# The list of steps of a second feed-forward exchanged for another list of the same steps

## Chip, core and metric

The kernel runs on one core of a Trainium2 chip. The metric is device time in microseconds from the start to the end of the program; less is better.

## What is computed

Windowed attention with a few global tokens, then a gated feed-forward (mish), then a second feed-forward whose gate is a cosine. Inputs and output are float32; x has 2176 rows of 512, the hidden width is 2048. The second feed-forward is the part that the change touches:

```python
    attn_out = _attn_ref(**attn_kwargs)
    x = np.ascontiguousarray(attn_out.transpose(0, 2, 1, 3)).reshape(B * S, H * D)
    x = _moe_ref(x=x, **moe_kwargs)
    return _moe2_ref(x=x, **moe2_kwargs)

def _moe2_ref(x, w_in, w_out):
    h = x @ w_in
    g = h * np.cos(h)
    return (g @ w_out).astype(np.float32)
```

## The kernel before

Every float32 matmul is made of three fp32r matmuls: each operand is split into a high and a low part, and low x high, high x high and high x low are added in PSUM.

The second feed-forward (`second`, L967) works in 24 stages: two halves p of the hidden width, three blocks b of tokens (2 x 384, 2 x 384, 2 x 320) and four groups j of 256 hidden columns, in that order. Stage s = 12p + 4b + j. In steps such as `P3:11` the number behind the colon is the stage. Within a stage the first matmul (x @ w_in) is done as seven products in place of eight, on sums and differences of the operands' quarters. The steps are:

- A, I, L (L925): form operand o of a token block (number behind the colon: block), cast its high part (I, letter a or d), subtract for the low part and store both to DRAM (L). The operands of one block at a time live in SBUF ("homes").
- P0 to P6 (L1021): product o, six matmuls (L1034) into one of two PSUM banks, chosen by (s + o) mod 2. In stage 4b + 3 a product also issues, on SyncE's queue, the reload of its operand for the next block (L957). At stages 8 to 11 some products also refill weights.
- E0 to E7 (L1048, L1051): copy (E0) or add (L1056, VectorE) a product from its bank, until the four quarters of h are made. A bank is free again when the sum that reads it is done.
- f0 to f6 and g0 to g6 (L1018, L841): the gate on the two column halves c = 0, 1: two ScalarE passes (f0), two VectorE passes (f1, f2), sine and square on ScalarE (f3), a VectorE pass (f4), a cast (f5, letter a or d), a subtraction on VectorE (f6). In the last stage they are cut in two once more (a, b for c = 0; d, c for c = 1). The scratch tile `k` is one for all.
- U0 to U5 and V0 to V5 (L1059): the second matmul (g @ w_out) of column half c = 0 (U) and 1 (V) for 128 tokens a: three matmuls (L1065) of 512 columns that add into PSUM sum a over the four groups j.
- Z0 to Z5 (L1071): empty sum a behind the last group: a copy to `part` for p = 0 (L1081, letter a or d), an add and the store of the output for p = 1 (L1083, L1084).
- X, Y (L1068): the weights of U or V of this stage are used up; for p = 0 at the last block the slot is refilled from DRAM (L433).
- R, S: one quarter each of the last two groups of the first feed-forward's second matmul (L1133).

The letter behind a step puts a copy or cast on ScalarE (a) or VectorE (d), in `move` (L346).

`ORDER2` (L71 to L128) is the order of all of these, written out. The program issues the steps exactly in this order (`tc.manual_schedule()`, L1208; the loop at L1095), so each engine and SyncE's queue gets its instructions in the order of the list and works them off in that order; between engines only data and buffers make one wait for another.

PSUM is full: eight banks. Sums a = 0 and 1 have a tile each, a = 2 and 3 are the two halves of one tile, a = 4 and 5 of another, and two tiles serve the products:

```python
    single = [late["ps"].tile([P, 512], F32, tag="acc", name="acc", bufs=4) for _ in range(4)]
    acc.extend(single[2:4] + [t[:, c] for t in (ps2, ps) for c in range(2)] + single[0:2])
```

In the profile the sums in halves are called `h`, the others `acc`; operands are `xo` and `xq` (o = 5, 6), `stage` where they are formed; h is `hs`, with `u` for partial sums; the gate is `w`, `gh`, `gl`; weights are `w`, `wb`, `wt`, in DRAM `scr`.

Of the kernel before, what the change touches and what calls it, by code (L numbers as in the profile page):

```python
# [68 lines left out]
"""  # L69

ORDER2 = """  # L71
    I6:0d L5:0 I0:1a P0:0 P1:0 E0:0d L6:0 P2:0 R:0 E1:0 I4:1a E2:0 L4:1 P3:0 P4:0 A5:1 E3:0 L0:1 E4:0 A3:1 f0:0
# [4 lines left out]
    P0:3 f0:2 P1:3 f1:2 V5:0 g5:1a E0:3a E1:3 U0:1 A6:1 P2:3 U4:1 f2:2 g6:1 f3:2 P3:3 I6:1d g0:2 U1:1 V1:1 E2:3
    f4:2 P4:3 L6:1 E3:3 E4:3 g1:2 U2:1 g2:2 U3:1 L4:2 U5:1 P5:3 P6:3 V3:1 f5:2a E6:3 g3:2 V0:1 f0:3 E7:3 A5:2 E5:3
    V2:1 P0:4 P1:4 g4:2 g5:2a E0:4a f6:2 V5:1 f1:3 A3:2 U2:2 E1:4 f2:3 P2:4 P3:4 E2:4 U5:2 P4:4 V4:1 U4:2 U0:2 f3:3
    g0:3 I0:2a g6:2 g1:3 E3:4 E4:4 g2:3 U1:2 f4:3 f0:4 g3:3 U3:2 f5:3a P6:4 P5:4 E6:4 E5:4 V5:2 L0:2 E7:4 V0:2 P0:5  # L80
    V4:2 E0:5a g4:3 f6:3 P1:5 g5:3a V3:2 f1:4 E1:5 I1:2d P2:5 P3:5 V1:2 U4:3 f2:4 V2:2 E2:5 I3:2a f3:4 E3:5 P5:5
    P4:5 g6:3 L1:2 L3:2 U0:3 V0:3 f4:4 g0:4 I5:2a U2:3 g1:4 U3:3 g2:4 A2:2 V4:3 V2:3 E4:5 P6:5 g3:4 E5:5 E6:5 E7:5
    g4:4 P0:6 P1:6 U1:3 Z4:3d f0:5 E0:6d U5:3 V1:3 f5:4a E1:6 f6:4 f1:5 A6:2 I2:2d Z0:3a f2:5 g5:4a P2:6 P3:6 E2:6
    f3:5 E3:6 V3:3 Z1:3a U0:4 V5:3 U4:4 P5:6 L5:2 g6:4 P4:6 f4:5 g0:5 V0:4 Z3:3d g1:5 U1:4 U3:4 E6:6 Z5:3a E4:6
    V3:4 E5:6 g2:5 f5:5a I6:2a L6:2 Z2:3a U5:4 P6:6 f0:6 f6:5 V1:4 E7:6 P0:7 U2:4 f1:6 P1:7 E0:7d g3:5 g4:5 L2:2
    P2:7 E1:7 V2:4 f2:6 V4:4 g5:5d E2:7 g0:6 U3:5 f3:6 P3:7 g6:5 P4:7 E3:7 E4:7 g1:6 f4:6 V5:4 g2:6 f5:6d f6:6 U1:5
    U4:5 f0:7 P5:7 g3:6 E6:7 P6:7 f1:7 U0:5 U2:5 E5:7 f2:7 V1:5 f3:7 E7:7 g4:6 V2:5 V0:5 P0:8 U5:5 P1:8 g5:6d E0:8a
    P2:8 f4:7 U0:6 V4:5 E1:8 E2:8 g6:6 P4:8 P3:8 g0:7 g1:7 V3:5 U4:6 E3:8 E4:8 P5:8 V5:5 U1:6 U2:6 g2:7 U5:6 E5:8
    E6:8 P6:8 P0:9 f0:8 g3:7 E7:8 f5:7d f6:7 U3:6 V5:6 f1:8 P1:9 E0:9d f2:8 g4:7 V1:6 V4:6 P2:9 g0:8 U1:7 E1:9
    g5:7d V3:6 g6:7 U4:7 g1:8 E2:9 f3:8 P3:9 P4:9 f4:8 U3:7 E3:9 P5:9 g2:8 V0:6 V2:6 U0:7 E5:9 E4:9 P6:9 f5:8d V3:7  # L90
    g3:8 f0:9 E6:9 E7:9 g4:8 U5:7 P0:10 P1:10 U2:7 f6:8 Z3:7a V1:7 E0:10d V2:7 P2:10 g5:8a E1:10 f1:9 f2:9 Z1:7d
# [6 lines left out]
    V2:10 f1:12 f2:12 E0:13a P1:13 g0:12 P2:13 E1:13 g5:11d P3:13 E2:13 g6:11 V1:10 P4:13 g1:12 V3:10 U1:11 X:8
    E3:13 E4:13 f3:12 V0:10 P5:13 P6:13 U2:11 g2:12 f4:12 E5:13 E6:13 g3:12 E7:13 P0:14 E0:14a P1:14 g4:12 E1:14
    f5:12a V2:11 f0:13 f6:12 P2:14 P3:14 U4:11 V4:11 V1:11 Z4:11a f1:13 U3:11 U0:11 E2:14 Z1:11a V3:11 Y:9 P4:14  # L100
    Z2:11a f2:13 U4:12 E3:14 E4:14 U5:12 P5:14 f3:13 g0:13 g5:12d V0:11 U1:12 U2:12 f4:13 g6:12 P6:14 g1:13 g2:13
# [5 lines left out]
    P0:17 V0:13 E7:16 E0:17a U0:14 P2:17 f5:15a U1:14 g4:15 P1:17 f6:15 U2:14 V1:14 f1:16 E1:17 V5:14 E2:17 f2:16
    P4:17 Y:11 P3:17 V4:14 V0:14 V3:14 E3:17 g5:15d g6:15 f3:16 f4:16 E4:17 P5:17 g0:16 V2:14 Y:20 g1:16 P6:17
    E5:17 E6:17 U3:15 V3:15 g2:16 U1:15 E7:17 U4:15 P0:18 E0:18d P1:18 g3:16 g4:16 U0:15 f5:16d E1:18 P2:18 f0:17
    P3:18 f6:16 V1:15 U5:15 V5:15 U2:15 f1:17 E2:18 f2:17 f3:17 Z1:15 V4:15 E3:18 P5:18 f4:17 P4:18 g0:17 Z4:15  # L110
# [1 line left out]
    g2:17 f5:17d f0:18 f6:17 V4:16 P0:19 V5:16 Z0:15 g3:17 E7:18 f1:18 g4:17 U2:16 U0:16 U5:17 g5:17d f2:18 E0:19a
    V3:16 P2:19 P1:19 U3:17 E1:19 f3:18 f4:18 E2:19 V0:16 P3:19 X:20 U4:17 E3:19 g0:18 g6:17 P4:19 V2:16 g1:18
    E4:19 P5:19 U2:17 g2:18 P6:19 E6:19 U1:17 E5:19 V4:17 f5:18a V5:17 E7:19 g3:18 P0:20 g4:18 f6:18 U0:17 E0:20d
    f0:19 g5:18d P1:20 f1:19 P2:20 E1:20 V0:17 f2:19 P3:20 E2:20 V2:17 f3:19 g6:18 U4:18 E3:20 P4:20 f4:19 P5:20
    E5:20 U5:18 E4:20 E6:20 V1:17 V5:18 V3:17 g0:19 P0:21 Y:22 P6:20 U2:18 g1:19 g2:19 U0:18 E7:20 f5:19d U3:18
    X:21 V3:18 U1:18 V1:18 g3:19 V0:18 P1:21 f0:20 f6:19 E0:21a f1:20 f2:20 P2:21 f3:20 g0:20 g4:19 E1:21 f4:20
    X:22 E2:21 g5:19a P3:21 U5:19 g6:19 V2:18 U1:19 V4:18 E3:21 U0:19 P5:21 E6:21 E5:21 g1:20 U2:19 P4:21 V2:19
    E4:21 g2:20 U4:19 P0:22 P6:21 g3:20 V5:19 U3:19 f0:21 f5:20d f6:20 E7:21 g4:20 P1:22 E0:22a f1:21 V3:19 f2:21
    E1:22 g5:20a Z2:19 X:23 g6:20 P2:22 P3:22 E2:22 V4:19 Z3:19 V1:19 g0:21 P4:22 f3:21 Z1:19 E3:22 Z4:19 V0:19  # L120
    P5:22 E4:22 U2:20 P6:22 U1:20 f4:21 Z0:19 g1:21 f5:21d E6:22 g2:21 U4:20 E5:22 V2:20 U0:20 f6:21 V0:20 P0:23
# [1143 lines left out]
```

## Time and profile before

| | us |
|---|---|
| median of 3 runs (873.9 to 876.3) | 875.49 |
| the profiled run | 875.59 |
| its span, first to last instruction | 873.8 |
| TensorE busy | 859.3 |
| VectorE busy | 731.0 |
| ScalarE busy | 485.4 |

The span is what the trace covers; the run's time has 1.8 us around it. Busy times of the engines overlap. A matmul's row begins when the engine takes it and its end is modelled, so rows of TensorE lie over each other: twelve matmuls in a row last less than twelve times one. An idle time stands in brackets behind an instruction, with the one whose end released it.

### The profile page before, as it was taken

Reading aid. Unit: us, or ns where it says so; the run is one execution under the profiler, and the core shown is the slowest. Engines: PE = TensorE matmul, PEld = TensorE weight load, DVE = VectorE, ACT = ScalarE, POOL = GpSimd, SP = SyncE. Lnnn points to the kernel's source line nnn. Section 1 sums busy time; section 2 is a strip of 40 time slices with the busy share of each in tenths; the row PEclk is TensorE's granted clock in tenths of the full one; section 3 lists DMA queues with packets and bytes.
Section 4 is the critical chain, followed back from the end, with each engine's and each line's share of the span. In section 5 each row is a group of like instructions: output and inputs, shape, how many; then the busy total and the mean of one; then the engine's idle time right before and its main releaser. Section 6 shows DMA issues by size and latency. Waiting matters only on the chain.

```text
span 873.8 us, 16116 instructions
## 1 busy us (share of the span) xinstructions
PE 859.3 (98%) x5995; PEld 790.5 (90%) x5995; DVE 731.0 (84%) x1499; ACT 485.4 (56%) x962; POOL 84.3 (10%) x137
## 2 busy tenths in 40 slices
...
GB/s 170 186 211 173 175 88 81 73 158 229 260 277 270 298 375 345 267 283 268 252 226 238 387 407 211 256 91 151 245 134 335 99 29 344 1 88 196 1 61 72
DMA packets 133886, 174.97 MB, mean 200 GB/s; under 512 B 77872, under 2 KB 100400, under 8 KB 133808
## 3 DMA queue, kind: packets, MB, share of 16 engines
...
## 4 chain that ended last, share of the span: by engine, by line
PE 81%; DMA 8%; DVE 8%; issue 1%; ACT 1%; SPq 0%; DVEq 0%; POOL 0%; POOLq 0%; ACTq 0%
PE acc L1034 17%; PE acc L1133 14%; PE h L1065 13%; PE acc L1065 7%; PE h L810 6%; PE h L812 6%; PE h L811 6%; DMA cs<-in_moe_w_out_dram 3%; DMA cs<-in_moe_w_in_dram 3%; PE s L572 3%; PE av L643 2%; PE ta L616 1%; DVE ca L240 1%; DMA op<-stage 1%; PE av L637 1%
## 5 line engine op out<-in xcount | busy, mean ns | idle before, releaser
L1133 PE MATMUL acc<-gh,w 128*128 128x384 f32 (+1 forms) x768 | 187.9, 328 | 0.0
L1133 PEld LDWEIGHTS acc<-gh,w 128*128 128x128 f32 x768 | 136.5, 189 | 0.0
L1133 PE MATMUL acc<-gl,w 128*128 128x384 f32 (+1 forms) x384 | 126.4, 329 | 3.0 <-DVE x L883 1.9
L810 PE MATMUL h<-x,w 128*128 128x384 f32 (+1 forms) x384 | 126.1, 328 | 0.7 <-DVE x L787 0.7
L812 PE MATMUL h<-x,w 128*128 128x384 f32 (+1 forms) x384 | 125.2, 326 | 0.0
L811 PE MATMUL h<-x,w 128*128 128x384 f32 (+1 forms) x384 | 125.2, 326 | 0.0
L1065 PE MATMUL h<-w,gh 128*128 128x512 f32 x352 | 109.7, 393 | 0.0
L1034 PE MATMUL acc<-xo,w 128*128 128x384 f32 (+1 forms) x402 | 76.3, 327 | 1.6 <-DVE hs L1056 1.6
L1065 PEld LDWEIGHTS h<-w,gh 128*128 128x128 f32 x352 | 66.1, 188 | 11.8
L1133 PEld LDWEIGHTS acc<-gl,w 128*128 128x128 f32 x384 | 72.5, 189 | 4.5 <-DVE x L883 2.2
L856 ACT ACTIVATE w<-w 128x768 f32<-128x768 f32 (+2 forms) x50 | 39.0, 781 | 63.2 <-DVE w L853 63.1
L1034 PEld LDWEIGHTS acc<-xo,w 128*128 128x128 f32 x402 | 68.1, 188 | 6.4 <-DVE hs L1056 2.7
L810 PEld LDWEIGHTS h<-x,w 128*128 128x128 f32 x384 | 72.1, 188 | 1.1 <-issue 1.0
L811 PEld LDWEIGHTS h<-x,w 128*128 128x128 f32 x384 | 72.1, 188 | 0.0
L812 PEld LDWEIGHTS h<-x,w 128*128 128x128 f32 x384 | 72.1, 188 | 0.0
L1065 PE MATMUL h<-w,gl 128*128 128x512 f32 x176 | 69.2, 393 | 1.9 <-DVE part L348 1.0
L1056 DVE TENSOR_TENSOR hs<-u,acc 128x384 f32<-128x384 f32 (+1 forms) x91 | 47.4, 526 | 27.9 <-PE acc L1034 26.5
L846 ACT ACTIVATE k<-hs,magic 128x768 f32<-128x768 f32 (+2 forms) x50 | 43.5, 871 | 49.1 <-DVE w L853 43.0
L1065 PE MATMUL acc<-w,gh 128*128 128x512 f32 x192 | 59.9, 393 | 0.0
L592 ACT ACTIVATE pr<-pr,nm 128x160 f32<-128x160 f32 x128 | 53.5, 423 | 8.8 <-DVE nm L589 8.0
L850 DVE SCALAR_TENSOR_TENSOR w<-k,hs 128x768 f32<-128x768 f32 (+2 forms) x50 | 44.1, 881 | 8.5 <-ACT k L847 6.8
L837 DVE TENSOR_TENSOR gl<-w,gh 128x768 fp32r<-128x768 f32 (+1 forms) x48 | 43.9, 916 | 7.1 <-ACT gh L833 7.1
...
## 6 DMA issues: line engine op xcount, KB each, us to landing
w<-scr SPq DMA_DIRECT2D x44, 512.0 KB, 7.1
scr<-co SPq DMA_DIRECT2D x31, 512.0 KB, 3.3
x<-x SPq DMA_DIRECT2D x32, 384.0 KB, 5.8
...
cs<-in_moe_w_in_dram SPq DMA_DIRECT2D x22, 512.0 KB, 4.3
cs<-in_moe_w_out_dram SPq DMA_DIRECT2D x22, 512.0 KB, 4.2
scr<-lab SPq DMA_DIRECT2D x21, 512.0 KB, 3.8
...
```

Source lines behind the costliest of these rows:

```text
L592: nc.scalar.activation(out=pr[:, i], in_=pr[:, i], func=AF.Exp, bias=nm[:, i:i + 1], scale=-1.0, accum_out=l[:, i:i + 1])
L810: nc.tensor.matmul(ps[:, c, 0:n], wh[:, k, :], xl, start=(k == 0), stop=False)
L811: nc.tensor.matmul(ps[:, c, 0:n], wh[:, k, :], xh, start=False, stop=False)
L812: nc.tensor.matmul(ps[:, c, 0:n], wl[:, k, :], xh, start=False, stop=(k == NK - 1))
L837: nc.vector.tensor_tensor(out=gl, in0=v["w"], in1=gh.bitcast(F32), op=ALU.subtract)
L846: nc.scalar.activation(out=k[:, y], in_=of("h")[:, z], func=AF.Identity, scale=INV2PI, bias=magic[:, 0:1])
L850: nc.vector.scalar_tensor_tensor(out=of("t")[:, z], in0=k[:, y], scalar=-C1, in1=of("h")[:, z], op0=ALU.mult, op1=ALU.add)
L856: nc.scalar.activation(out=of("t")[:, z], in_=of("t")[:, z], func=AF.Sin, scale=0.5)
L1034: nc.tensor.matmul(to, l[:, i + c], r, start=c == 0 and m == 0, stop=c == 1 and m == 2)
L1056: nc.vector.tensor_tensor(out=of[out](), in0=of[x](), in1=bank(s, o), op=ALU.add)
L1065: nc.tensor.matmul(singles()[a], l[:, a * P:(a + 1) * P], r, start=(j, c) == (0, 0) and m == 0, stop=(j, c) == (3, 1) and m == 2)
L1133: nc.tensor.matmul(o[:, 0:n], w[:, a * P:(a + 1) * P], r[:, c, :], start=(not goes_on and g == 0 and m == 0), stop=(not stays and g == G - ...
```

## The change

`ORDER2` is replaced as a whole. Both lists have 1079 steps, and each step of one is in the other; their order differs, and for some the letter a or d. Nothing else in the program changes, the attention's list `ORDER` included. Of the lists those lines that hold the steps spoken of below:

```diff
-    I6:0d L5:0 I0:1a P0:0 P1:0 E0:0d L6:0 P2:0 R:0 E1:0 I4:1a E2:0 L4:1 P3:0 P4:0 A5:1 E3:0 L0:1 E4:0 A3:1 f0:0
-    A2:1 R:1 f1:0 P5:0 R:2 S:0 E6:0 E5:0 f2:0 f3:0 S:1 S:2 P6:0 f4:0 E7:0 f5:0d P0:1 E0:1a f6:0 I3:1a R:3 S:3 g0:0
-    P2:1 P1:1 E1:1 P3:1 E2:1 I1:1a E3:1 g1:0 U2:0 P4:1 P5:1 g2:0 E4:1 L1:1 f0:1 U3:0 E5:1 P6:1 E6:1 L3:1 U5:0 g3:0
...
-    E2:10 f3:9 P3:10 E3:10 g0:9 f4:9 P4:10 P5:10 V4:7 E4:10 g6:8 V5:7 V0:7 U3:8 P6:10 g1:9 g2:9 V3:8 Z2:7d E6:10
-    E5:10 E7:10 Z0:7a Z4:7d P0:11 f5:9a P1:11 U1:8 U0:8 g3:9 f0:10 E0:11a g4:9 f6:9 U2:8 E1:11 P3:11 U4:8 g5:9a
...
-    f4:11 g3:11 P6:12 P5:12 U0:10 E6:12 E5:12 f5:11d f0:12 U3:10 f6:11 E7:12 Z5:7d Y:8 P0:13 g4:11 V4:10 U2:10
...
-    V5:12 E5:14 g3:13 E6:14 P0:15 E7:14 Z3:11d Z0:11d V2:12 U3:12 P1:15 E0:15d f5:13a f0:14 U0:12 X:9 g4:13 f6:13
-    V0:12 f1:14 E1:15 P2:15 E2:15 V3:12 V1:12 f2:14 P3:15 g5:13d Y:10 E3:15 U5:13 P4:15 g6:13 g0:14 P5:15 g1:14
...
-    Z3:15 Y:21 V2:15 U3:16 E4:18 Z5:15 g5:16a g6:16 V0:15 E5:18 E6:18 Z2:15 P6:18 U1:16 g1:17 V1:16 U4:16 U5:16
...
-    V4:21 P6:23 a0:23 g4:22 a1:23 b0:23 E6:23 E7:23 U3:22 V1:21 b1:23 a2:23 U2:21 V0:21 b2:23 g5:22d U0:22 a3:23
-    c0:23 g6:22 b3:23 V2:21 U4:22 d0:23 c1:23 b4:23 V0:22 U2:22 a4:23 b5:23d U1:22 a5:23a d1:23 V4:22 V2:22 d2:23
...
-    Z5:19 U3:23 V0:23 Z2:23 Z4:23 U1:23 V1:23 Z0:23 Y:23 V3:23 Z1:23 Z3:23
+    P0:0 I6:0a L6:0 E0:0a P1:0 P2:0 E1:0 I4:1d E2:0 L5:0 P3:0 P4:0 E3:0 R:0 P5:0 L4:1 E4:0 A5:1 P6:0 E5:0 E6:0 f0:0
...
+    P2:1 P3:1 E2:1 P4:1 f6:0 E3:1 g3:0 U1:0 E4:1 g4:0 I3:1a P5:1 E6:1 U5:0 f0:1 E5:1 P6:1 f1:1 E7:1 P0:2 f2:1 P1:2
...
+    Z2:3a f3:5 Z3:3a E2:6 Z4:3a E3:6 P4:6 E4:6 P5:6 P6:6 E6:6 V5:3 f4:5 V0:3 g0:5 g6:4 U4:4 E7:6 I2:2a U3:4 Z5:3a
+    Z0:3a g1:5 L2:2 f5:5d V3:4 U5:4 U0:4 E5:6 P0:7 U2:4 g2:5 V4:4 g3:5 g4:5 P1:7 E0:7a V2:4 f6:5 E1:7 U1:4 f0:6
...
+    f4:6 L6:2 V1:5 P5:7 g4:6 f0:7 E6:7 V0:5 U5:5 P6:7 U4:5 g5:6a E5:7 P0:8 f5:6d V3:5 f6:6 E7:7 f1:7 f2:7 g6:6 g0:7
...
+    P6:9 U4:7 V5:7 U3:7 f0:9 f5:8d P0:10 E7:9 f6:8 f1:9 f2:9 E0:10a g5:8d V2:7 V4:7 f3:9 f4:9 P1:10 P2:10 Z2:7a
+    V3:7 E1:10 g0:9 V1:7 g6:8 Z4:7a E2:10 P3:10 P4:10 V0:7 E3:10 Z1:7d E4:10 U2:8 g1:9 f5:9a P5:10 Z3:7a P6:10 U1:8
...
+    V0:9 f6:10 g2:10 U2:9 P5:11 V2:9 E4:11 g3:10 E5:11 U4:9 g4:10 E6:11 V4:9 P6:11 g5:10d Z5:7d f0:11 P0:12 E7:11
+    f1:11 V1:9 P1:12 E0:12d f2:11 E1:12 P2:12 E2:12 V3:9 P3:12 P4:12 E3:12 P5:12 g0:11 g6:10 U4:10 X:9 U2:10 E4:12
...
+    P3:14 E2:14 E3:14 U3:11 P4:14 E4:14 P5:14 P6:14 g5:12d E5:14 Z1:11a E6:14 V3:11 E7:14 P0:15 g0:13 Z2:11d f5:13a
+    U0:12 g6:12 Z3:11a U3:12 P1:15 U1:12 E0:15a X:11 f6:13 U2:12 g1:13 Y:11 Z4:11a g2:13 g3:13 U4:12 V4:12 g4:13
...
+    g1:17 U5:16 f3:17 P4:18 P5:18 V5:16 Z3:15 g2:17 E4:18 X:21 f4:17 V4:15 Z1:15 g3:17 V2:15 E6:18 P6:18 U0:16
...
+    P5:23 b1:23 V2:21 b2:23 g4:22 U2:22 g5:22a a1:23 E5:23 a2:23 V1:21 E6:23 b3:23 g6:22 V0:21 a3:23 c0:23 U0:22
+    E7:23 b4:23 Z5:19 U1:22 d0:23 V3:21 d1:23 c1:23 a4:23 V4:21 V0:22 b5:23d U4:22 c2:23 U3:22 V3:22 d2:23 c3:23
...
+    U1:23 Z2:23 Z3:23 U0:23 V0:23 V1:23 V4:23 Z0:23 Z1:23 Z4:23
```

## Rows read from the trace of the kernel before

**Rows 1.** Page: busy us, share of the span, instructions of each engine.
```profile
PE 859.3 (98%) x5995; PEld 790.5 (90%) x5995; DVE 731.0 (84%) x1499; ACT 485.4 (56%) x962; POOL 84.3 (10%) x137
```

**Rows 2.** Busy time by stretch: length, each engine's us, PEclk, DMA share, GB/s.
```profile
530.00:560.00 30.00, 30.00 (x153) 26.95 (x152) 29.19 (x42) 19.95 (x25) 0.00 (x0) 1.00 0.70 265
```

**Rows 3.** Chain that ended last: start, us to the next piece, what.
```profile
538.20 1.39 PE h L1065 x6
539.59 2.10 PE acc L1034 x12
...
808.98 1.75 PE acc L1034 x12
```

**Rows 4.** Waits of TensorE, 495 to 874 us: us in total, times, longest.
```profile
PE acc L1034 <- DVE hs L1056: 2.4, 2, 1.6
PE h L1065 <- DVE part L348: 1.0, 1, 1.0
PE h L1065 <- DMA w<-scr: 0.7, 1, 0.7
PE h L1065 <- DVE part L1083: 0.3, 1, 0.3
```

**Rows 5.** Timeline around U3:0 and P6:1: start, us, engine, line, [idle before <-releaser].
```profile
521.74 0.96 DVE L850 SCALAR_TENSOR_TENSOR w<-k,hs 128x768 f32<-128x768 f32 x1 [1.00 <-ACT k L847]
...
522.51 0.39 PE L1065 MATMUL h<-w,gl 128*128 128x512 f32 x1
...
524.21 1.32 PE L1034 MATMUL acc<-xq,w 128*128 128x384 f32 x6 [0.84 <-DVE hs L1056]
```

**Rows 6.** Waits of ScalarE, 495 to 874 us: us in total, times, longest.
```profile
ACT stage L350 <- DMA op<-stage: 8.4, 6, 3.7
```

**Rows 7.** Timeline: V3:8 begins, finish Z2:7, P0:11 begins.
```profile
654.75 0.39 PE L1065 MATMUL h<-w,gl 128*128 128x512 f32 x1
...
655.64 0.69 DVE L348 COPY part<-h 128x512 f32<-128x512 f32 x1 [1.92 <-PE h L1065]
...
657.18 2.02 PE L1034 MATMUL acc<-xo,w 128*128 128x320 f32 x12 [1.57 <-DVE hs L1056]
```

**Rows 8.** Timeline: P0:13 and V4:10; P4:18 and V2:15.
```profile
685.99 1.23 PE L1034 MATMUL acc<-xo,w 128*128 128x384 f32 x6
...
688.21 0.50 PE L1065 MATMUL h<-w,gl 128*128 128x512 f32 x1 [0.99 <-DVE part L348]
...
773.50 1.21 PE L1034 MATMUL acc<-xo,wt 128*128 128x384 f32 x6
...
774.97 0.50 PE L1065 MATMUL h<-w,gl 128*128 128x512 f32 x1 [0.27 <-DVE part L1083]
```

**Rows 9.** Timeline: P3:15 and U5:13.
```profile
724.12 1.21 PE L1034 MATMUL acc<-xo,w 128*128 128x384 f32 x6
...
725.99 0.50 PE L1065 MATMUL h<-w,gl 128*128 128x512 f32 x1 [0.66 <-DMA w<-scr]
```

**Rows 10.** DMA issues, 495 to 874 us: count, KB each, median us to landing.
```profile
w<-scr SPq DMA_DIRECT2D x24, 512.0 KB, 7.3
...
xq<-op SPq DMA_DIRECT2D x12, 384.0 KB, 6.6
```

**Rows 11.** Groups by line and shape, 495 to 874 us: busy us, mean ns | idle before.
```profile
L348 DVE COPY part<-h 128x512 f32<-128x512 f32 x6 | 4.1, 685 | 1.9 <-PE h L1065 1.9
...
L350 ACT COPY part<-h 128x512 f32<-128x512 f32 x5 | 2.9, 583 | 7.8 <-PE h L1065 7.8
```

**Rows 12.** Timeline at the end: the last gate products (d6, c6), V4:23.
```profile
863.00 1.10 DVE L866 TENSOR_TENSOR gl<-w,gh 128x320 fp32r<-128x320 f32 x2
...
865.20 0.39 PE L1065 MATMUL h<-w,gl 128*128 128x512 f32 x1
```

**Rows 13.** Groups by line and shape: a half-width pass on VectorE.
```profile
L866 DVE TENSOR_TENSOR gl<-w,gh 128x320 fp32r<-128x320 f32 x4 | 1.9, 486 | 0.1
```

**Rows 14.** Waits of SyncE's queue, 495 to 874 us: us in total, times, longest.
```profile
SPq L965 <- DMA op<-stage: 6.7, 1, 6.7
```

More of the change, by code (lines that the diff above doesn't have):

```diff
@@ L77 @@
[L77 to L91, printed above, removed]
@@ L92 @@
-    E2:10 f3:9 P3:10 E3:10 g0:9 f4:9 P4:10 P5:10 V4:7 E4:10 g6:8 V5:7 V0:7 U3:8 P6:10 g1:9 g2:9 V3:8 Z2:7d E6:10
-    E5:10 E7:10 Z0:7a Z4:7d P0:11 f5:9a P1:11 U1:8 U0:8 g3:9 f0:10 E0:11a g4:9 f6:9 U2:8 E1:11 P3:11 U4:8 g5:9a
-    P2:11 f1:10 V1:8 E2:11 f2:10 V4:8 E3:11 g6:9 P4:11 V0:8 g0:10 U3:9 U1:9 P5:11 U0:9 g1:10 E4:11 f3:10 g2:10
-    P6:11 U4:9 g3:10 g4:10 V4:9 f4:10 V2:8 f5:10a V1:9 f0:11 E5:11 E6:11 P0:12 E7:11 V0:9 f6:10 E0:12a P1:12 P2:12
-    f1:11 U4:10 f2:11 U2:9 E1:12 E2:12 P3:12 g5:10a g6:10 P4:12 E3:12 V2:9 g0:11 V3:9 E4:12 g1:11 g2:11 U1:10 f3:11
@@ L97 @@
-    f4:11 g3:11 P6:12 P5:12 U0:10 E6:12 E5:12 f5:11d f0:12 U3:10 f6:11 E7:12 Z5:7d Y:8 P0:13 g4:11 V4:10 U2:10
[L98 to L101, printed above, removed]
@@ L102 @@
-    V5:12 E5:14 g3:13 E6:14 P0:15 E7:14 Z3:11d Z0:11d V2:12 U3:12 P1:15 E0:15d f5:13a f0:14 U0:12 X:9 g4:13 f6:13
-    V0:12 f1:14 E1:15 P2:15 E2:15 V3:12 V1:12 f2:14 P3:15 g5:13d Y:10 E3:15 U5:13 P4:15 g6:13 g0:14 P5:15 g1:14
-    U0:13 U1:13 E4:15 f3:14 f4:14 E6:15 g2:14 E5:15 U3:13 P6:15 E7:15 g3:14 g4:14 P0:16 U2:13 V2:13 V4:12 f5:14a
-    P1:16 E0:16d P2:16 V1:13 U4:13 E1:16 V4:13 f0:15 X:10 g5:14a P3:16 X:11 f6:14 E2:16 f1:15 f2:15 P4:16 g0:15
-    E3:16 f3:15 g6:14 P5:16 U4:14 V5:13 E4:16 V3:13 g1:15 U5:14 U3:14 g2:15 f0:16 P6:16 f4:15 g3:15 E6:16 E5:16
@@ L107 @@
[L107 to L110, printed above, removed]
-    Z3:15 Y:21 V2:15 U3:16 E4:18 Z5:15 g5:16a g6:16 V0:15 E5:18 E6:18 Z2:15 P6:18 U1:16 g1:17 V1:16 U4:16 U5:16
@@ L112 @@
[L112 to L121, printed above, removed]
@@ L127 @@
-    Z5:19 U3:23 V0:23 Z2:23 Z4:23 U1:23 V1:23 Z0:23 Y:23 V3:23 Z1:23 Z3:23
+    P0:0 I6:0a L6:0 E0:0a P1:0 P2:0 E1:0 I4:1d E2:0 L5:0 P3:0 P4:0 E3:0 R:0 P5:0 L4:1 E4:0 A5:1 P6:0 E5:0 E6:0 f0:0
+    E7:0 f1:0 I0:1a f2:0 R:1 P0:1 A3:1 L0:1 f3:0 S:0 P1:1 S:1 g0:0 f4:0 R:2 R:3 E0:1a f5:0a g1:0 E1:1 g2:0 S:2 S:3
+    P2:1 P3:1 E2:1 P4:1 f6:0 E3:1 g3:0 U1:0 E4:1 g4:0 I3:1a P5:1 E6:1 U5:0 f0:1 E5:1 P6:1 f1:1 E7:1 P0:2 f2:1 P1:2
+    g5:0a L3:1 g6:0 E0:2a E1:2 g0:1 P2:2 U0:0 I1:1a E2:2 f3:1 U2:0 L1:1 P3:2 g1:1 P4:2 V2:0 E3:2 E4:2 A2:1 g2:1
@@ new lines @@
+    V0:0 P5:2 f4:1 I5:1a P6:2 f0:2 f5:1a E6:2 L5:1 I2:1a U4:0 U3:0 E5:2 E7:2 V4:0 V3:0 g3:1 L2:1 P0:3 V5:0 f6:1
+    g4:1 E0:3a f1:2 V1:0 A6:1 P1:3 g5:1a I6:1a P2:3 U0:1 E1:3 U2:1 P3:3 f2:2 E2:3 g0:2 g6:1 g1:2 f3:2 P4:3 U4:1
+    V4:1 E3:3 I4:2a P5:3 g2:2 U3:1 E4:3 g3:2 U5:1 V3:1 f4:2 L6:1 f5:2a E6:3 f6:2 P6:3 f0:3 E5:3 g4:2 E7:3 f1:3 V5:1
+    L4:2 V0:1 U0:2 U1:1 f2:3 P0:4 E0:4d P1:4 E1:4 P2:4 g5:2d V2:1 g0:3 E2:4 P3:4 V1:1 g6:2 P4:4 f3:3 f4:3 f5:3a
+    U3:2 A5:2 g1:3 E3:4 U2:2 g2:3 V3:2 E4:4 P5:4 E5:4 E6:4 f0:4 P6:4 U4:2 g3:3 U5:2 P0:5 f6:3 A3:2 E7:4 I0:2d I3:2a
@@ new lines @@
+    f1:4 V5:2 g4:3 U3:3 P1:5 E0:5a U1:2 f2:4 f3:4 E1:5 V1:2 L0:2 P2:5 P3:5 g5:3a V0:2 L3:2 I1:2a E2:5 V2:2 E3:5
+    P4:5 P5:5 f4:4 g6:3 U2:3 U1:3 E4:5 g0:4 g1:4 U5:3 V4:2 V2:3 E5:5 E6:5 I5:2a g2:4 P6:5 L1:2 U4:3 f5:4a A2:2 g3:4
+    P0:6 f6:4 E7:5 L5:2 V1:3 E0:6a U0:3 g4:4 f0:5 A6:2 Z1:3a P1:6 g5:4d E1:6 f1:5 P2:6 P3:6 V3:3 f2:5 I6:2a V4:3
+    Z2:3a f3:5 Z3:3a E2:6 Z4:3a E3:6 P4:6 E4:6 P5:6 P6:6 E6:6 V5:3 f4:5 V0:3 g0:5 g6:4 U4:4 E7:6 I2:2a U3:4 Z5:3a
+    Z0:3a g1:5 L2:2 f5:5d V3:4 U5:4 U0:4 E5:6 P0:7 U2:4 g2:5 V4:4 g3:5 g4:5 P1:7 E0:7a V2:4 f6:5 E1:7 U1:4 f0:6
@@ new lines @@
+    V5:4 V1:4 U2:5 f1:6 f2:6 g5:5a P2:7 E2:7 V0:4 P3:7 g0:6 g6:5 g1:6 f3:6 g2:6 U0:5 P4:7 E3:7 g3:6 U1:5 E4:7 U3:5
+    f4:6 L6:2 V1:5 P5:7 g4:6 f0:7 E6:7 V0:5 U5:5 P6:7 U4:5 g5:6a E5:7 P0:8 f5:6d V3:5 f6:6 E7:7 f1:7 f2:7 g6:6 g0:7
+    V5:5 E0:8d P1:8 U3:6 P2:8 E1:8 g1:7 P3:8 E2:8 U5:6 f3:7 g2:7 E3:8 P4:8 g3:7 P5:8 E4:8 f4:7 V2:5 E6:8 E5:8 P6:8
+    U1:6 E7:8 U2:6 P0:9 E0:9d V4:5 P1:9 V2:6 f5:7a g4:7 E1:9 P2:9 V1:6 f6:7 f0:8 f1:8 U0:6 U4:6 P3:9 V5:6 U1:7 E2:9
+    f2:8 f3:8 P4:9 E3:9 P5:9 f4:8 g5:7a E4:9 U5:7 g0:8 g6:7 g1:8 U2:7 V0:6 E6:9 V4:6 g2:8 g3:8 V3:6 g4:8 E5:9 U0:7
```

32 lines of the change are left out of this document (27 added, 5 removed).

## Prediction

> **What bounds the kernel now.** I read the page first, then the busy time by stretch, then TensorE's waits, then the stretches around each wait. The page gives TensorE 859.3 of 873.8 us [rows 1]: it is the bound. "Busy" there says too little, since ends of matmuls are modelled; what counts is the distance from one start to the next. The chain shows the distances of an undisturbed stretch [rows 3]: six unit matmuls of 512 columns take 1.39 us to the next start, so a step U or V (three) costs 0.68 to 0.69 us; twelve product matmuls of 384 columns take 2.10, so a step P costs 1.05; of 320 columns 0.88.
>
> The list rules the stretch from the first P at 501 us to the end. Where a step starts later than these distances allow, TensorE lost time. Over 50 ns was lost at 21 places, the first at 522.51, the last at 774.97 [rows 5, 8], 6.8 us in all. Most of it lies at six spots: at 522.51, 654.75, 685.99, 724.12 and 773.50, which stand in [rows 5, 7, 8, 9], and a small one at 716.54. The waits that the trace itself puts down there are 4.4 us [rows 4], less than what the starts show, since a matmul that waits for its weights is not listed. The ceiling of any new order of the same steps is about 6.8 us. VectorE is second: 731.0 us over the span [rows 1], and 29.19 of the 30 from 530 to 560 [rows 2]. Early in the list it has no slack. Granted clock is 1.00 there, the level of 2.4 GHz [rows 2].
>
> **The change part by part.** The two lists hold the same 1079 steps: every P, E, f, g, U, V, Z, X, Y, A, I, L occurs once in both, so matmuls, weights and transfers are equal in number and size. Only order differs, and the engine of some moves: those on VectorE (letter d) go from 45 to 39.
>
> *Ties.* The sums of a = 2, 3 and of a = 4, 5 are halves of one PSUM tile each. At 655.64 the copy of finish Z2:7 had waited 1.92 us for TensorE although V2:7 was long done; it started when V3:8, the other half, was through, which stands just before it in the old list [rows 7]. VectorE's sums behind it came late, and P0:11 started 2.43 us after V3:8 instead of 0.69: 1.74 lost, and 0.11 in the next step. The other direction is at 688.21 and 774.97: V4:10 and V2:15 write a half while the finish of its partner (Z5:7, Z3:15) is still queued on VectorE [rows 8]: 2.22 for 1.05 and 1.47 for 1.05, so 1.17 and 0.42 lost, 0.11 more after each. V2:12 behind Z3:11 lost 0.31 in the same way. Sum: 1.85 + 1.28 + 0.53 + 0.31 = 4.0 us. In the new list Z2:7 no longer follows a V3:8; V4:10 stands over 7.7 us of TensorE's steps behind Z5:7, and Z3:15 finds its tile idle for 11 us. I take the 4.0 us as gone.
>
> The new list has tight ties of its own. I counted TensorE's steps from the last write of either half before a finish to the next write after it. Shortest are U4:4 to U5:4 around Z5:3 with 1.4 us (the units U3:4 and V3:4), V3:11 to U3:12 around Z2:11 and Z3:11 with 1.7, V2:7 to V3:7 and U2:8 to U3:8 with 2.4. A finish costs 0.583 on ScalarE or 0.685 on VectorE [rows 11], so each fits if its engine is there in time, and the old list had such distances of 0.7 to 2.8 us with losses from 0 to 0.5. Bounds 0 and 1.5 us for all; I take 0.5, near the lower end, because ScalarE does most of them and waits often.
>
> *The queue of ScalarE at the start.* In the old list I3:1a stands ahead of g0:0. Its tile is free only when a store has landed; ScalarE stood 8.4 us in all before such casts, up to 3.7 [rows 6]. So g0:0 came late, VectorE waited 1.00 us for it at 521.74, the sum E4:1 behind came late, and P6:1 started 1.70 instead of 0.69 us after U3:0: 1.0 lost, 0.1 after [rows 5]. In the new list I3:1a stands behind g0:0, g3:0 and E4:1. Gain 1.1 us. The price if the cover is gone: ScalarE then holds f0:1 instead, whose results are wanted some ten steps later; nothing on TensorE waits soon.
>
> *Transfers.* X:9 refills a weight slot, and in the old list U5:13 wants it 4.1 us of TensorE's steps later (two P, three units). Such a refill takes 7.3 us (median) [rows 10]; it landed late, and U5:13 and the next step lost 0.95 us [rows 9]. In the new list no refill by X or Y has less than 28 us before its first use. Gain 0.95. On the other side the operand reloads of P5 and P6 at steps 7 and 11 have 9.4 to 10.2 us of TensorE's work before their use, where the old list gives 12.1 to 14.8. They take 6.6 us (median) [rows 10], so 3 us stay. P6:7's is the tightest: L6:2, whose store it must wait for, stands only 3.1 us of steps before P6:7. Bounds 0 and 1.5; I take 0.1, since VectorE reaches that place with over 5 us more lead than in the old list (below).
>
> *Banks.* A product waits until the sum of the product before the last has left its bank. Mean cover is 3.1 us in both lists. Counting VectorE's work listed from that product to its sum against the cover, the worst excess is 3.2 us in the old list and 2.5 in the new, and all excesses add up to 39 and 29 us. In the old list nearly all of them were absorbed by lead, some 0.1 us at a time being lost. Bounds 0 and 1.0 us; I take 0.5, hardly below the 0.6 of the old one's small places.
>
> *VectorE's load.* Counted with the rows' durations, up to P3:7 the old list gives TensorE 103.6 us and VectorE 103.1, the new one 104.3 and 98.7. That speaks for the new list where [rows 2] show VectorE full.
>
> *The end.* In the old list the last gate products were done at 864.10 and V4:23, the first unit to need the last of them, began at 865.20: 1.1 us to spare [rows 12]. From the last product to that unit TensorE had 17 units (11.6 us) as cover and VectorE 11.2 us of listed work (half-width steps at 0.49 [rows 13], of which there are sixteen). In the new list P5:23 is last, V2:23 has 18 units (12.3 us) before it, and VectorE 12.5 us: Z5:19 (0.68), E5:23 (0.48) and two half casts (0.32 each) come in, one cast of g5:22 (0.49) goes to ScalarE. Margin 1.1 + 0.7 - 1.3 = 0.5 us; the same count for U2:23 leaves 0.1. Bounds 0 and 1.0; I take 0.3. Behind the last matmul nothing changes: three finishes of 0.68 us follow three units of 0.68, in both.
>
> *Sum.* None of the bounds goes below nothing, since TensorE does not run under its steady distances [rows 3]. Removed: 4.0 + 1.1 + 0.95 = 6.05 us. Added: ties 0.5, reloads 0.1, end 0.3; the old small places (0.6) stay as 0.5 in the banks. Net 6.05 + 0.6 - 0.5 - 0.9 = 5.25; I give back 0.5 for transfers and casts that meet in ways no row of before shows (bounds 0 and 1.5): 4.75 us.
>
> *The page that speaks against it.* [Rows 7] show a copy of one half waiting for matmuls into the other. The Trainium skill, PSUM — Partial Sum Buffer, section Specifications (TRN2), says that ScalarE and VectorE can both access PSUM at full bandwidth as long as no bank collides, and its Terms make a bank 2 KiB per partition, which is one half of such a tile. By that rule no hardware asks for this wait, and a list that respects the tie would gain nothing from it, which is rival (a); by the row the wait is there, set by the program. I go by the row.
>
> **The rivals.** (a) *The ties were not the cause.* If the copy at 655.64 and the writes at 688.21 and 774.97 were late through VectorE's queue and not through the other half, the 4.0 us come back elsewhere; left are 1.1 + 0.95, less 1.4 of new losses: 873.8 - 0.65 + 1.8 = 875.0. For it: VectorE is loaded throughout. Against it: it stood idle 1.92 us at the first of them.
> (b) *Every wait goes.* 873.8 - 6.8 + 1.8 = 868.8. Against it: the small places.
> (c) *Slower: the store of L6:2 holds P6:7's reload.* SyncE's queue has waited 6.7 us for such a store before a reload [rows 14]. If VectorE reaches L6:2 late by d, the store is out at d + 1.1, landed at d + 7.8, the two reloads at about d + 14.9 counted from the place in the list; P6:8 wants them at 3.1 + 10.4 = 13.5. The loss is 1.4 + d. With the other new losses it outweighs the 6.05 us from about d = 4 on; with d = 6 the time is 873.8 - 4.75 + 7.4 + 1.8 = 878.2. Against it: the lead above.
> (d) *The list does less than it says:* half of the ties return at places like Z5:3: 873.8 - 2.75 + 1.8 = 872.9.
>
> **How the numbers follow.** The profiled run took 875.59 us, 1.8 over its span and 0.1 over the median of the three runs (875.49), so both serve alike. Forecast 873.8 - 4.75 + 1.8 = 870.9 us (rounded up). Chances: forecast 0.55, (b) 0.13, (d) 0.14, (a) 0.12, (c) 0.06. The unknown costs make 868.8 to 874.0 around the forecast; (a) at 875.0 lies outside, and half of it with (c) and a run below (b) are what I leave out: 868.6 to 874.8. A difference of 0.3% (2.6 us) is about what a measurement can tell from none: below 872.9 lie the forecast, (b) and half of (d), 0.75; within it the rest of (d), (a) and a part of (c), 0.20; above 878.1 0.05.
>
> **What would show it.** Right: TensorE's waits in this stretch shrink from 4.4 us to under 2, none is for a copy of "part", none for a refill; busy TensorE stays at 859 or falls by under 1 us; no 1 us gap around U3:0 and P6:1. Wrong: TensorE waits for DMA at P5 or P6 of step 8 or 12, for "part" around U5:4, U3:12 or V3:7, or for "gl" behind the last product.

## The result and the profile after

The new list takes 868.0 us (median of 6 runs, 866.01 to 869.41) against 875.05 (6 runs, 873.9 to 876.3): ratio 0.9918, 95% interval 0.9902 to 0.9934. So it is faster by 7.05 us, where 4.6 was forecast, and lies 0.6 us below the range. The profiled run took 868.88 us, its span is 867.1 (before 873.8).

The page of the new list, busy us by engine (before: [rows 1]):

```profile
PE 855.7 (99%) x5995; PEld 789.6 (91%) x5995; DVE 725.8 (84%) x1492; ACT 490.7 (57%) x969; POOL 84.0 (10%) x137
```

As many matmuls as before; seven instructions have gone from VectorE to ScalarE. (The count of letters was six fewer; a cast of o = 5 or 6 in the first block is two instructions.) Busy TensorE fell by 3.6 us, more than the "under 1" that I had named. Of these, 2.4 us lie behind the first P: rows also grow while a matmul waits (0.50 us in place of 0.39 at 688.21, [rows 8]). Another 1.2 lie ahead of it, where both programs are the same. So busy time is no measure of the work.

No matmul waits any more in the stretch of the list (495 us to the end; before: [rows 4], 4.4 us). Weight loads have waits of their own: before, seven of them waited for a sum of h and others for `part`, `u` or a transfer; now one waits. The first row is of before, the second of after; columns: us in total, times, longest:

```profile
PEld acc L1034 <- DVE hs L1056: 4.3, 7, 2.0
```

```profile
PEld acc L1034 <- DVE hs L1056: 0.5, 1, 0.5
```

The two traces can be laid side by side step by step, since the same steps run. I took the distance from the start of each step to the start of the next and subtracted the steady one (0.680 us for a unit, 1.040 for a product of 384 columns, 0.875 of 320). Worked from all starts of the two traces (where a step R or S stands between two starts, the place is left out):

| | old list | new list |
|---|---|---|
| first P starts at | 501.12 | 501.02 |
| last V ends at | 870.12 | 863.27 |
| stretch between | 369.00 | 362.25 |
| places over 0.05 us | 21, together 7.21 | 2, together 0.33 |
| from there to the end of the span | 3.68 | 3.82 |

So the 6.7 us between the spans lie in the stretch, and there in the 21 places: all are gone, and two small ones are new. The ones of the ties (Z2:7, Z5:7, Z3:15, Z3:11 and, not counted as one in the prediction, Z3:7 at 645.98) come to 4.27 us with the step behind each, P6:1 to 1.13, the refill to 0.96, the rest to 0.85.

Each narrow place that I had feared held. Timeline of the new list around Z2:11 and Z3:11, one of the tightest (V3:11 starts at 707.66, U3:12 at 710.12; line 348 and line 350 are the two finishes):

```profile
707.66 0.39 PE L1065 MATMUL h<-w,gl 128*128 128x512 f32 x1
...
708.56 0.69 DVE L348 COPY part<-h 128x512 f32<-128x512 f32 x1
709.30 0.58 ACT L350 COPY part<-h 128x512 f32<-128x512 f32 x1
...
710.12 0.40 PE L1065 MATMUL h<-w,gl 128*128 128x512 f32 x1
```

Z3:11 is done at 709.88, 0.24 us before U3:12 writes the tile. Z2:7 was done 0.17 us before V3:7, the closest of all, and Z5:3 0.57 us before U5:4. Z5:15, which I had not counted among the shortest, was done 0.25 us before U5:16. At the end (before: [rows 12]) the last gate product and V2:23, the unit that needs it:

```profile
857.35 0.49 DVE L866 TENSOR_TENSOR gl<-w,gh 128x320 fp32r<-128x320 f32 x1 [0.58 <-ACT gh L350]
...
858.35 0.39 PE L1065 MATMUL h<-w,gl 128*128 128x512 f32 x1
```

It is done at 857.84, 0.5 us ahead: the margin that I had worked out, and no loss. ScalarE's waits for a store before a cast shrank from [rows 6] to this:

```profile
ACT stage L350 <- DMA op<-stage: 3.0, 2, 2.2
```

And the store of L6:2 with the reloads behind it (queue of SyncE; the four loads in the second line are those of P5:7 and P6:7), and P6:8, which wants them:

```profile
610.60 0.32 SPq L955 DMA_DIRECT2D op<-stage  x1
611.02 5.38 SPq L962 DMA_DIRECT2D xq<-op  x4
...
622.70 1.04 PE L1034 MATMUL acc<-xq,w 128*128 128x320 f32 x6
```

The store landed at 615.14, the last reload at 619.62: 3.1 us before P6:8.

### The profile page after: what moved, and what is told of

It is laid out like the page before. It is cut to its first block, busy times and chain, and to the rows that moved or that the text cites. A ratio compares the mean times of both kernels' runs of the same rounds, so it can differ in the third digit from the quotient of the medians.

```text
span 867.1 us, 16120 instructions
## 1 busy us (share of the span) xinstructions
PE 855.7 (99%) x5995; PEld 789.6 (91%) x5995; DVE 725.8 (84%) x1492; ACT 490.7 (57%) x969; POOL 84.0 (10%) x137
## 4 chain that ended last, share of the span: by engine, by line
PE 83%; DMA 7%; DVE 7%; ACT 1%; issue 1%; SPq 0%; DVEq 0%; POOL 0%; POOLq 0%; ACTq 0%
PE acc L1034 18%; PE h L1065 14%; PE acc L1133 14%; PE acc L1065 8%; PE h L810 5%; PE h L812 5%; PE h L811 5%; DMA cs<-in_moe_w_out_dram 4%; DMA cs<-in_moe_w_in_dram 3%; PE s L572 2%; PE av L643 2%; DVE ca L240 2%; PE ta L616 1%; PE av L637 1%; PE avg L720 1%; PE h L1034 1%
## 5 line engine op out<-in xcount | busy, mean ns | idle before, releaser
L1034 PE MATMUL acc<-xo,w 128*128 128x384 f32 (+1 forms) x402 | 76.1, 327 | 0.0
L1034 PEld LDWEIGHTS acc<-xo,w 128*128 128x128 f32 x402 | 68.7, 188 | 4.7 <-DVE hs L1056 0.5
L860 DVE SCALAR_TENSOR_TENSOR w<-w,hs 128x768 f32<-128x768 f32 (+2 forms) x50 | 43.9, 880 | 14.0 <-ACT w L857 13.8
L866 DVE TENSOR_TENSOR gl<-w,gh 128x768 fp32r<-128x768 f32 (+2 forms) x50 | 43.8, 879 | 9.4 <-ACT gh L350 9.1
```

Source lines behind the costliest of these rows:

```text
L860: nc.vector.scalar_tensor_tensor(out=of("t")[:, z], in0=of("t")[:, z], scalar=1.0, in1=of("h")[:, z], op0=ALU.subtract, op1=ALU.mult, reve ...
L866: nc.vector.tensor_tensor(out=of("gl")[:, z], in0=of("t")[:, z], in1=of("gh")[:, z].bitcast(F32), op=ALU.subtract)
L1034: nc.tensor.matmul(to, l[:, i + c], r, start=c == 0 and m == 0, stop=c == 1 and m == 2)
```

## The experiments

Theory: places in the list carry the gain, above all five finishes on tied halves (4.0 us), then a cast that stood too early (1.1) and a refill that stood too late (0.95). Rivals: the ties were not what made VectorE and TensorE wait; or the new order as a whole, with its lighter VectorE, is what counts. The first experiments therefore start from the old list and move a few steps. "Stretch" is from the first P to the last V as above. In some of these kernels the list takes a line more or less, so that line numbers differ by one from those of before (L1033 or L1035 for L1034, and so on).

| kernel | time (us, median) | ratio to before | stretch | places over 0.05 us, sum |
|---|---|---|---|---|
| before | 875.05 | | 369.00 | 7.21 |
| after | 868.0 | 0.9918 (0.9902 to 0.9934) | 362.25 | 0.33 |
| old_ties | 873.47 | 0.9967 (0.9953 to 0.9981) | 366.34 | 4.51 |
| old_queue | 875.03, one run | | 368.78 | 6.92 |
| old_refill | 874.37, one run | | 368.20 | 6.37 |
| old_all | 870.53 | 0.9934 (0.9912 to 0.9956) | 364.55 | 2.53 |
| old_untied | 872.68 | 0.9966 (0.9950 to 0.9981) | 365.14 | 3.23 |
| old_few | 871.94 | 0.9948 (0.9928 to 0.9968) | 363.89 | 1.84 |
| new_late_store | 870.47, one run | | 364.14 | 2.22 |
| new_cast_first | 876.78, one run | | 370.71 | 8.84 |
| new_sum | 868.13, one run | | 361.99 | 0.00 |
| new_evac_sum | 865.42 | 0.9887 (0.9868 to 0.9907) | 361.90 | 0.00 |

A ratio is taken against runs of before made beside those of the kernel, so it is not the quotient of two times of this table. The stretch is the sharper measure here: the part ahead of the first P, which no list touches, took 500.2 to 503.7 us in the eleven traces in which it is the same program.

**old_ties.** Five finishes moved, each to where no write to the other half is near:

```diff
-    ... g4:8 U5:7 P0:10 P1:10 U2:7 f6:8 Z3:7a V1:7 ... E2:10 ... g2:9 V3:8 Z2:7d
+    ... g4:8 Z3:7a U5:7 P0:10 P1:10 U2:7 f6:8 V1:7 ... E2:10 Z2:7d ... g2:9 V3:8
-    ... P4:12 E3:12 ... E7:12 Z5:7d ... E4:14 ... E7:14 Z3:11d ... E0:18d ... Z4:15 Z3:15
+    ... P4:12 E3:12 Z5:7d ... E7:12 ... E4:14 Z3:11d ... E7:14 ... E0:18d Z3:15 ... Z4:15
```

> The old list with five finishes moved to places where no write to the other half of their tile stands close before or behind them: Z3:7, Z2:7, Z5:7, Z3:11, Z3:15. Theory (the tie of the two halves is what cost): the stretch from the first P to the last V falls from 369.0 us by about 4.0 to 365.0, no wait of TensorE for a copy or add of part, waits around P6:1 (1.0) and U5:13 (0.8) stay; time about 871. Rival (VectorE's queue was late whatever the tie): the finishes are moved in VectorE's queue without making it shorter, so the stretch stays above 368 and the gaps turn up elsewhere.

Measured: all five places are gone (4.27 us). Three things took some of it back. The moved finishes made VectorE late for P0:15 (0.46) and P3:18 (0.54), and with everything earlier the refill came 0.45 later for U5:13. TensorE's waits, 495 us to the end:

```profile
PE acc L1033 <- DVE hs L1055: 1.1, 2, 0.9
PE h L1064 <- DMA w<-scr: 1.1, 1, 1.1
PE acc L1033 <- DVE u L1055: 0.2, 1, 0.2
```

No wait for "part" is among them. The stretch fell by 2.66, not 4.0: the theory holds for the cause, but a moved finish still takes its 0.69 us of an engine, and a sum behind it can come late. For P3:18 and Z3:15 old_few shows this below; for P0:15 old_untied does, where Z3:11 stands behind it as before and P0:15 is on time.

**old_untied.** This changes no order at all. The two tiles of two halves become four tiles, in the same banks:

```diff
-        ps = late["psa"].tile([P, 2, 512], F32, tag="a", name="h")
+        late["psa_stack"].close()
+        psb = ctx.enter_context(tc.tile_pool(name="psb", bufs=1, space=bass.MemoryType.PSUM))
+        half = [psb.tile([P, 512], F32, tag=f"b{i}", name=f"half{i}") for i in range(4)]
...
-        ps2 = late["psa"].tile([P, 2, 512], F32, tag="a", name="h")
...
-                acc.extend(single[2:4] + [t[:, c] for t in (ps2, ps) for c in range(2)] + single[0:2])
+                acc.extend(single[2:4] + [half[i] for i in (2, 3, 0, 1)] + single[0:2])
...
-                return (ps, ps2)[i][:, 0, 0:n_of(s)]
+                return half[2 * i][:, 0:n_of(s)]
...
```

> The old list, unchanged, with the two PSUM tiles of two halves each replaced by four tiles of one half each in the same banks. Theory (the halves are tied by the program alone): the waits at Z2:7, V4:10, V2:12, V2:15 and V2:7, 4.3 us of TensorE's time, go without a step being moved; the wait for the refill at U5:13 grows by up to 0.5, as it did with the finishes moved; stretch 364.7 to 365.2. Rival (VectorE's queue or the chip's banks make them wait): stretch 368.5 or more.

Measured: 365.14, as expected. Timeline from the end of U3:8 to P0:11 (before: [rows 7]). U3:8 and V3:8 write the half of a = 3; the copy at 653.76 is Z2:7, which reads the half of a = 2, and the one at 655.56 is Z4:7:

```profile
653.55 0.61 PE L1066 MATMUL half<-w,gh 128*128 128x512 f32 x2
653.76 0.68 DVE L348 COPY part<-half 128x512 f32<-128x512 f32 x1
...
654.88 0.39 PE L1066 MATMUL half<-w,gl 128*128 128x512 f32 x1
...
655.56 0.69 DVE L348 COPY part<-half 128x512 f32<-128x512 f32 x1
655.57 1.92 PE L1035 MATMUL acc<-xo,w 128*128 128x320 f32 x12
```

P0:11 starts 0.69 us after V3:8, its steady distance; before it was 2.43. Z2:7 no longer waits for V3:8: it runs 1.1 us ahead of it, and its first 0.4 us lie under the last matmuls of U3:8 into the other half (653.76 to 654.16; ends on TensorE are modelled). So the tie is a bookkeeping of the program: both halves count as one tile. Here VectorE read one half while TensorE wrote the other. This agrees with the page cited in the prediction (the Trainium skill, PSUM — Partial Sum Buffer, Terms), by which two engines collide when they are in one bank at the same time; and the row of before was right that the wait was there. Both were true, of different things. Splitting the tiles brings 3.9 us of the stretch with no step moved; the new list gets there by order.

**old_refill.** X:9, X:10 behind X:8, Y:11 behind Y:10:

```diff
-    ... U0:12 X:9 g4:13 ... P3:15 g5:13d Y:10 E3:15 ...
+    ... X:8 X:9 X:10 ... U0:12 g4:13 ... P3:15 g5:13d Y:10 Y:11 E3:15 ...
```

> The old list with X:9 and X:10 moved up behind X:8, and Y:11 behind Y:10. Theory (the refill came late because it stands late in the list): U5:13 starts without a wait, stretch 368.0 us (0.95 less). Rival (SyncE's queue and the reloads of operands delay it anyway, or the earlier refill delays them): the wait stays or turns up at another load; stretch 368.5 or above.

Measured: the wait at U5:13 is gone with its follower (0.96), the stretch 0.80 shorter; nothing else moved by more than 0.1. The step holds as priced.

**old_queue.** I3:1a behind g0:0:

```diff
-    ... E0:1a f6:0 I3:1a R:3 S:3 g0:0
+    ... E0:1a f6:0 R:3 S:3 g0:0 I3:1a
```

> The old list with one step moved: I3:1a behind g0:0 instead of three steps ahead of it. Theory (the cast waits for a store and holds g0:0 on ScalarE's queue): P6:1 starts within 0.1 us of its steady distance after U3:0, stretch 367.9 us (1.1 less). Rival (E4:1 is late because VectorE is full there): P6:1 still loses 0.5 us or more, stretch 368.5 or above.

Measured: P6:1 is on time (1.13 gone), but 0.80 turned up at P2:2: the stretch is 0.22 shorter, not 1.1. Timeline of ScalarE and TensorE there:

```profile
527.74 0.83 ACT L349 CAST stage<-x 128x768 fp32r<-128x768 f32 x1 [1.38 <-DMA op<-stage]
...
528.48 0.47 ACT L349 COPY u<-acc 128x384 f32<-128x384 f32 x1
529.00 0.45 PE L1033 MATMUL acc<-xo,wb 128*128 128x384 f32 x1 [0.62 <-ACT u L349]
```

The cast here is I2:1a. It waits 1.38 us (0.61 before) for the store of I1:1, which took 4.0 us from issue to landing (3.3 before), and behind it stands E0:2a, the copy that frees the bank of P2:2. The theory was right on the cause; what the prediction had added, that nothing on TensorE waits soon if the cover is gone, was wrong. The new list puts that cast (I1:1a there) behind E0:2a.

**old_all.** All three edits together.

> The old list with all three edits (five finishes, I3:1a, X:9, X:10, Y:11), eight or nine steps moved of 1079. Theory: the gains add, 6.0 us: stretch 363.0, time about 869, within 1 us of the new list; the many places of about 0.1 us go too if they only follow the large ones, then 362.4. Rival (the new order of the other thousand steps carries part of the gain): stretch 364 to 366.

Measured: 364.55, inside the rival's range. Yet the five ties, P6:1 and the refill are all gone; what is left is what the edits themselves brought (P2:2 1.09 with its follower, P0:15 0.46, P3:18 0.56) and 0.4 elsewhere, of it 0.28 at P4:9. The places of about 0.1 us in the first stages (526 to 555 us) went too, but TensorE had been held 0.95 us at P2:2 ahead of them; old_few shows what they are without that.

**old_few.** As old_all, with I2:1a behind E0:2a, Z3:11 on ScalarE (Z3:11a), Z3:15 behind E1:18.

> The old list with the three edits and three touches where they had left gaps: I2:1a behind E0:2a (ScalarE held that copy, and P2:2 waited), Z3:11 on ScalarE, Z3:15 behind E1:18. Theory (a handful of places carry the whole gain): the 1.1 us at P2:2 and the 1.0 us at P0:15 and P3:18 go; stretch 362.5 to 363.0, within 0.7 us of the new list. Rival (the rest of the new order matters too): 364 or more.

Measured: 363.89, above what I expected and 0.1 below the rival's bound. P2:2 and P3:18 are free; P0:15 still loses 0.6 and P5:18 0.37. Z3:11 on ScalarE did not help P0:15: the gate passes on ScalarE stand behind it now, and VectorE waits for one of them ahead of the sum that frees the bank of P0:15:

```profile
710.28 0.96 DVE L860 SCALAR_TENSOR_TENSOR w<-w,hs 128x768 f32<-128x768 f32 x1 [0.64 <-ACT w L857]
```

(The profiled run took 873.0 us: its first P came late, at 503.65. Where the other runs, 868.25 to 872.14, lost their time is not shown.) Ten of 1079 steps moved give 5.1 of the 6.75 us.

The rest is not only a matter of better places for the finishes. With P2:2 free, the small places of the first stages are back: 0.11 at V0:0, 0.29 at P6:2 and 0.10 at P1:4, the latter two with as much as before. And P4:9 loses 0.28 us, with the step behind it, in all seven traces of the old list and its edits, whichever of the large places is gone, and in none of the five of the new list. Its weight load waits for a sum; in before:

```profile
636.65 0.88 PEld L1034 LDWEIGHTS acc<-xo,wt 128*128 128x128 f32 x6 [0.28 <-DVE u L1056]
```

So the order of other steps carries a part of the gain too, at least the 0.28 us of P4:9.

**new_cast_first.** The new list with one step put back:

```diff
-    ... S:1 g0:0 f4:0 R:2 R:3 E0:1a ... E4:1 g4:0 I3:1a P5:1
+    ... S:1 I3:1a g0:0 f4:0 R:2 R:3 E0:1a ... E4:1 g4:0 P5:1
```

> The new list with one step moved back: I3:1a ahead of g0:0, where the old list has it. Theory (the cast waits for its store at the head of ScalarE's queue, and the gate behind it, the sum and the product follow): TensorE loses about 1 us between stage 0 and stage 2, stretch 363.3. Rival (it was VectorE's load, which is lighter in the new list): no loss over 0.2 us, stretch 362.3.

Measured: 8.46 us lost, far more than either said. Timeline: the cast, the copy E0:1a, and P4:1:

```profile
518.82 0.83 ACT L350 CAST stage<-x 128x768 fp32r<-128x768 f32 x1 [5.85 <-DMA op<-stage]
...
521.36 0.46 ACT L350 COPY u<-h 128x384 f32<-128x384 f32 x1
...
525.10 1.33 PE L1034 MATMUL acc<-xo,wt 128*128 128x384 f32 x3 [6.06 <-DVE u L1056]
```

In the old list E0:1a stands ahead of the cast; here it stands behind it, waits 5.85 us with it, and P4:1 needs a bank at the end of that chain of sums. And the granted clock falls to half while TensorE waits, so that it goes on at half clock. Busy time by stretch; the last three columns are PEclk, DMA share, GB/s:

```profile
510.00:517.00 7.00, 7.00 (x48) 7.00 (x47) 4.67 (x7) 2.56 (x3) 0.00 (x0) 1.00 1.04 407
517.00:523.00 6.00, 2.04 (x12) 1.72 (x10) 1.51 (x3) 3.70 (x5) 0.00 (x0) 1.00 1.02 419
523.00:530.00 7.00, 4.90 (x14) 4.63 (x15) 4.80 (x8) 3.64 (x5) 0.00 (x0) 0.51 0.18 69
530.00:537.00 7.00, 7.00 (x39) 6.59 (x39) 6.51 (x10) 4.39 (x6) 0.00 (x0) 1.00 0.24 98
```

The wait itself is 6.2 us; the three steps at half clock (1.2 GHz), P4:1, U1:0 and P5:1, cost another 2.3. It is one run, but the loss is read from the starts in its trace.

**new_late_store.** This puts a price on rival (c): L6:2 directly before P6:7.

```diff
-    ... f4:6 L6:2 V1:5 P5:7 g4:6 f0:7 E6:7 V0:5 U5:5 P6:7
+    ... f4:6 V1:5 P5:7 g4:6 f0:7 E6:7 V0:5 U5:5 L6:2 P6:7
```

> The new list with L6:2, and so its store, moved from three products and units ahead to directly before P6:7. As the prediction priced it (store 6.7 us, reload 6.6 us behind it): P6:8 waits about 3.3 us, stretch 365.6. By the durations of the new trace at that place (store 4.2, reloads 4.4, 3.1 us to spare): about 1.3 us to spare, no wait, stretch 362.3.

Measured: P6:8 lost 1.65 us, half of the one and more than the other; the stretch is 364.14. Counted from the first P, the store went out 1.7 us later than in the new list, not 3.1 (VectorE ran ahead of the list). But it took 5.8 us to land where it had taken 4.2, the second reload's issue took 1.3 us, and the last reload landed 6.5 us behind the store where it had been 4.5:

```profile
611.55 0.33 SPq L955 DMA_DIRECT2D op<-stage  x1
617.71 1.94 SPq L962 DMA_DIRECT2D xq<-op  x2
...
624.16 0.70 PE L1034 MATMUL acc<-xq,w 128*128 128x320 f32 x3 [1.39 <-DMA xq<-op]
```

So the mechanism of (c) is real, and the new list is 3.1 us away from it. My count from the durations of the new trace had left 1.3 us to spare: the transfers did not keep their durations when the store moved.

**new_sum.** The one loss left, P0:16 behind E5:15: E5:15 moved ahead of f6:14.

```diff
-    ... E6:15 f6:14 U3:13 P6:15 E5:15 V1:13 f0:15 P0:16
+    ... E6:15 E5:15 f6:14 U3:13 P6:15 V1:13 f0:15 P0:16
```

> The new list with one step moved: E5:15 behind E6:15, ahead of f6:14. The trace of the new list shows one loss left, P0:16 waiting for E5:15, which stood behind f6:14 (0.95 us) on VectorE: 0.33 us with the step after it. Theory (a sum behind a gate step on VectorE): it goes, stretch 361.9. Rival (the bank is not what it waits for): 362.3.

Measured: 361.99, no place over 0.05 us is left. In the stretch of the list TensorE is at its steady distances throughout.

**new_evac_sum.** What is left of TensorE's waits lies ahead of the list. The largest there in each of the traces so far, shown for the new list from 260 us on:

```profile
PE acc L1133 <- DVE x L883: 2.3, 2, 1.9
```

This kernel is new_sum with one more edit:

```diff
-                if rate:
+                if rate and i not in (17, 19):
                     conv.dve()
...
+            if rate and i in (17, 19):
+                conv.dve()
             if rate:
                 conv.act()
```

> As before, and in the first feed-forward the weight conversion's VectorE steps of groups 17 and 19 are issued behind the second matmul and its evacuation instead of ahead of it. In every trace TensorE stands 1.9 us at about 265 us for an evacuation queued behind those conversion steps, and in most of them its granted clock is 0.50 for 3.4 us about a microsecond after it goes on. Theory: the wait goes and with it the half clock; the first P starts about 1.9 us earlier than without (at 498.5 to 499.5), time 865 to 866.5. Rival (the conversion is what bounds that stretch, its transfers above all): the wait turns up within 20 us, the first P stays at 500 to 501.5, time about 868.

Measured: the wait is gone, the first P starts at 497.81, the time is 865.42 us (865.17 to 867.86), ratio to before 0.9887. From 260 to 300 us TensorE is busy 39.38 us where the new list alone has 37.69:

```profile
260.00:300.00 40.00, 39.38 (x227) 38.30 (x226) 37.74 (x71) 16.37 (x27) 0.00 (x0) 1.00 0.85 292
```

It has the shortest median of the study; its interval overlaps that of the new list alone, so that it is faster than this is read from the trace and not from the times. Its trace shows no half clock at that place, but neither do five others that have the wait, so that part of the theory stays open.

## Why the prediction was wrong

- *The bound and the ceiling* were right: TensorE's steady distances, 6.8 us by the starts (7.2 with one constant distance for each kind of step), and nearly all of it went (the stretch is 6.75 shorter). That is rival (b), to which I gave 0.13.
- *Ties*: right in cause (old_untied) and size: 4.0 forecast, 4.27 measured; Z3:7's 0.28 stood among my "small places". Rival (a) is out.
- *The queue of ScalarE*: right in cause, 1.1 forecast, 1.13 removed. The price if the cover is gone ("nothing on TensorE waits soon") was wrong: 0.8 in old_queue, 8.5 in new_cast_first. A copy that frees a bank stood behind the cast. In the new list the cast did not wait, so this error did not move the forecast.
- *The refill*: right, 0.95 forecast, 0.96 removed.
- *What the new list adds* is the step that failed. I booked 0.5 for narrow ties, 0.5 for banks, 0.3 for the end, 0.1 for reloads and 0.5 as a give-back: 1.9 us. Measured: 0.33, all of it at a bank (P0:16 waits for E5:15). The end shows it best: my own count left 0.5 and 0.1 us of margin, the trace shows 0.5, and yet I took 0.3 as loss. Ties, reloads and end came out as margins, and I booked a chance of a cost for each as if it were a cost, and added the chances up. The give-back had no row under it at all.
- *The small places* are the 0.5 for banks: I kept 0.5 of the old list's 0.6. They measure 0.85 and all went. They were not just followers of the large ones: P4:9 and, in old_few, P6:2 and P1:4 stay when the large ones are gone. The new order frees them; which of its steps does is not shown.
- *The range*: the profiled run, 868.88, lies inside, the median 0.6 below. Of the 2.9 us between the forecast and the median, 2.0 lie between the forecast and the profiled run (870.9 to 868.9), 1.6 of them by the added terms (1.9 booked, 0.33 measured), and 0.9 is what the profiled run stands above the median. The sum worked from one execution was set equal to a median, but the first part alone, with the same instructions, ends between 500.2 and 503.7 us from trace to trace. A low end for the forecast that every wait goes (868.8) left 0.2 for that.
